# Resident spectra, a third weight buffer and finer pacing in a convolution-plus-MLP kernel

## The chip, the cores and the metric

The kernel runs on one core of a Trainium2 chip. The metric is the device time of one execution in microseconds (us). Before the change the median of three runs is 520.09 us (519.62 to 520.41); the profiled run took 519.61 us, of which 517.8 us lie between the first and the last instruction of the program.

## The reference

The inputs are bfloat16; S = 2048 rows, D = 576 columns, F = 4608. One block of a gated sequence model is computed: an adaptive layer norm, a causal convolution over the whole sequence with a gate, a second adaptive layer norm, and a gated MLP.

```python
def _A_ref(q, k, v, shift_k, ssm_k, ssm_D):
    ...  # k_shift: four shifted copies of k, weighted by shift_k
    kv = k_shift * v
    ...  # y: causal convolution of each column of kv with a filter of 2048 taps (by FFT)
    y = y + kv * ssm_D[None, None, :]
    return q * y

def _B_ref(x, w1, w3, w2):
    gate = jnp.einsum('bsd,df->bsf', x, w1)
    up = jnp.einsum('bsd,df->bsf', x, w3)
    h = _silu(gate) * up
    return jnp.einsum('bsf,fd->bsd', h, w2)

mod = (_silu(c) @ w_mod)            # six rows: sa, ca, ga, sb, cb, gb
h = _layernorm(x) * (1 + ca) + sa
x = x + ga * _A_ref(h, A_k, A_v, A_shift_k, A_ssm_k, A_ssm_D)
h = _layernorm(x) * (1 + cb) + sb
x = x + gb * _B_ref(h, B_w1, B_w3, B_w2)
```

## The kernel before

The 2048 rows are cut into 8 blocks of 256 rows for the convolution and into 4 row blocks r of 512 rows for the MLP. The convolution is done block against block: each block s of kv gets a spectrum X[s], each block of the filter a spectrum V[s] (both 128 x 3456 bfloat16 in SBUF, 864 KB), by matmuls with cosine and sine matrices (`forward2`, lines 304 and 318). The spectrum of output block s is z[s], the sum of X[i]*V[s-i] over i. Each product of that sum is made by `pair` on VectorE: a multiply (L420; L414 for the first) and an add (L422). `real_parts` (L534 to L541) folds z, `inverse` (L554) turns it back by matmuls, `residual` (L568, L569) adds it to x.

The MLP of row block r runs on TensorE: `stream` makes gate and up (L949 over four full chunks of D, L960 over the last 64 rows), ScalarE evicts them (L968, L970), VectorE multiplies (L971), and `down` multiplies by w2 (L1061) in two column halves h, whose results VectorE takes out of PSUM with `og` (L1078). Row block 3 uses `stream_halves` (L1016).

While TensorE works on row block r, the convolution of blocks 2r+2 and 2r+3 is fed in as a generator of small steps, each with a cost in us. After each piece of MLP work `advance` takes as many steps as the budget allows. A negative cost in `mix` is a wait that is filled with steps of another generator.

```python
HEAD = 8
HEAD_PACE = 1.8
CONV_US = (72.0, 97.0, 108.0)
FIRST_DUE = 12.0
# pools: X has 3 buffers, V has 4, wst (w1/w3 chunks) 2 + wst[2], which is also the memory of w2 (w2m)

def x_sums(self, s):
    X = self.X[s]
    self.nc.vector.tensor_add(X[:, 0:6:3, :], X[:, 1:6:3, :], X[:, 2:6:3, :])
    if 3 < s < NBLK - 2:
        self.keep_x(s)                    # X[4], X[5] are written to DRAM
    yield 0.75

def old_x(self, i, s):
    return self.X[i] if s == 2 or s == 4 and i > 0 else self.get("X", i)   # get: 864 KB from DRAM

def old_v(self, i, s):
    return self.V[i] if i >= s - 4 and s < 6 or i >= 4 else self.get("V", i)

def ln_sums(self, src, i, ssum, ssq, col=None):
    col = i if col is None else col
    for func, scale, out in ((ACT.Copy, -1.0 / D, ssum), (ACT.Square, D ** -0.5, ssq)):
        junk = self.lnp.tile([P, D], BF16, name="junk", tag="junk")
        self.nc.scalar.activation(junk[:], src[:, i, :], func, scale=scale, accum_out=out[:, col:col + 1])  # L452

def outcome(self, s, fill, waits, between=None, quick=False):
    def steps():
        yield self.real_parts(s)
        yield -waits[0]
        ...                               # inverse(s, 0), inverse(s, 1) on TensorE, y on ScalarE
        yield -waits[1]
        self.residual(s, y)
        yield 1.5
        if between is not None:
            between()
        ...
            for i in range(2):
                with self.behind(nc.scalar):
                    self.ln_sums(self.xo[s], i, *sums)
                yield 0.0
            yield -waits[2] / 2
            stats = self.ln_var(*sums, "l2")
            yield -waits[2] / 2
            scales = self.ln_shift(*stats)
            yield -3.0
            for cc in range(2):
                self.normed_act(s, cc, *scales)
                yield -1.0
        yield -waits[3]
    yield from self.mix(steps(), fill)

def conv(self, s0):                       # s0 = 2, 4, 6; s1 = s0 + 1
    ...
    def old():
        V, X = self.old_v(s0 - 1, s0), self.old_x(1, s0)
        yield from self.pair(X, V, s0, s0 == 2)
        for j in range(2, s0):
            X = self.old_x(j, s0)
            yield from self.pair(X, V, s1)
            V = self.old_v(s0 - j, s0)
            yield from self.pair(X, V, s0)
        self.V1 = V
        yield from self.gate_stats(s0)
        yield from self.kv_rows(s0)
        ...
    yield from self.mix(filters(), old())
    ...                                   # X0, V0, x_spectrum(s0), X1; pairs with block s0
    def more():
        yield from self.pair(self.X1, self.V[s0], s1, True)
        yield from self.pair(self.X[s0], self.V1, s1)
    def others():
        yield from self.kv_rows(s1)
        self.gate_shift(s1)
        yield from self.mix(self.x_spectrum(s1), more())
        yield from self.x_sums(s1)
    yield from self.outcome(s0, others(), (5.0, 4.5, 6.0, 0.0), lambda: self.gate_rows(s1))
    yield from self.pair(self.X[s1], V0, s1)
    ...
    yield from self.outcome(s1, ahead, (5.0, 4.5, 5.0, 0.0), lambda: self.turn_all(s0))

def advance(self, cost):
    self.due += cost
    while self.due > 0 and self.steps is not None:
        c = next(self.steps, None)
        if c is None:
            self.steps = None
            break
        self.due -= c
        self.spent += c

# down: after chunk 5 of the second half, the rest of the steps, then the transposes of the next rows
                if h == 1 and f0 // W2C == 5 and r + 1 < NRB:
                    self.end()
                    self.turn_all(2 * r + 3)

# row_blocks, r > 0: w1/w3 chunk fc of row block r goes to one of two buffers
                jobs = [(fc, 0, RB, (r + fc) % 2, ...) for fc in range(NF // FC)]
```

Of the kernel before, what the change touches and what calls it, by code (L numbers as in the profile page):

```python
# [34 lines left out]
HEAD = 8  # L35
HEAD_PACE = 1.8
EPS = 1e-5
# [9 lines left out]
class _Kernel:  # L47
    def __init__(self, ctx, tc, q, k, v, shift_k, ssm_k, ssm_D, w1, w3, w2, c, w_mod, out):
# [20 lines left out]
        self.w13, self.kept = {}, {}  # L69
        self.gets = 0  # L70

    def ps(self, shape=(P, 2, 512), dtype=F32):
# [283 lines left out]
    def x_sums(self, s):  # L356
        X = self.X[s]
        self.nc.vector.tensor_add(X[:, 0:6:3, :], X[:, 1:6:3, :], X[:, 2:6:3, :])
        if 3 < s < NBLK - 2:
            self.keep_x(s)  # L360
        yield 0.75
# [71 lines left out]
    def old_x(self, i, s):  # L433

        return self.X[i] if s == 2 or s == 4 and i > 0 else self.get("X", i)

# [11 lines left out]
    def ln_sums(self, src, i, ssum, ssq, col=None):  # L448
        col = i if col is None else col
        for func, scale, out in ((ACT.Copy, -1.0 / D, ssum), (ACT.Square, D ** -0.5, ssq)):  # L450
            junk = self.lnp.tile([P, D], BF16, name="junk", tag="junk")
            self.nc.scalar.activation(junk[:], src[:, i, :], func, scale=scale, accum_out=out[:, col:col + 1])  # L452

# [189 lines left out]
    def first_block(self):  # L643
# [53 lines left out]
        self.mod_piece(2)  # L697
        self.ln_sums(x1, 0, sums[0], sums[1], 0)
        scales = [self.ln_shift(*self.ln_var(*sums, "l1")), (rstd, nmr)]
# [51 lines left out]
    def outcome(self, s, fill, waits, between=None, quick=False):  # L751


        def steps():
# [67 lines left out]
    def conv(self, s0):  # L822
# [13 lines left out]
        def old():  # L836
            V, X = self.old_v(s0 - 1, s0), self.old_x(1, s0)
            yield from self.pair(X, V, s0, s0 == 2)
            for j in range(2, s0):
                X = self.old_x(j, s0)  # L840
                yield from self.pair(X, V, s1)
                V = self.old_v(s0 - j, s0)
                yield from self.pair(X, V, s0)
            self.V1 = V
            yield from self.gate_stats(s0)
# [7 lines left out]
        def beside():  # L853
# [236 lines left out]
    def end(self):  # L1090
        self.advance(1e9)

# [22 lines left out]
    def row_blocks(self, n1):  # L1115
        for r in range(NRB):
# [17 lines left out]
            else:  # L1134
                spills = {1: (self.keep_x, 1), 2: (self.keep_v, 0), 4: (self.keep_v, 1)} if r == 1 else {}
                jobs = [(fc, 0, RB, (r + fc) % 2, (lambda f, i: lambda: f(i))(*spills[fc]) if fc in spills else None)
                        for fc in range(NF // FC)]
# [59 lines left out]
```

## Time and profile before

| view | value |
|---|---|
| median time | 520.09 us |
| span of the profiled run, instructions | 517.8 us, 9255 |
| TensorE (PE) busy | 498.4 us, 96% |
| VectorE (DVE) busy | 345.5 us, 67% |
| ScalarE (ACT) busy | 292.9 us, 57% |
| DMA moved | 107.80 MB, mean 208 GB/s |
| stages, from the lines in the timeline | start 0 to 35 us; row block 0 to 172; row block 1 to 292; row block 2 to 408.6; row block 3 to the end |

A stage is told by where the MLP lines L949 and L1061 begin and end. TensorE runs its instructions in program order, so a matmul of the convolution that waits for VectorE also stops the MLP matmuls behind it. A busy share says how much of a stretch an engine worked; what a change may save on TensorE is first of all its idle time.

### The profile page before, as it was taken

What the parts mean: (1) busy time and instruction counts of PE and PEld (TensorE: products, weight loads), DVE (VectorE), ACT (ScalarE), POOL (GpSimd) and SP (SyncE); (2) the same over time, 40 slices, a digit from 0 to 9 for tenths busy, and PEclk for the clock granted to TensorE, in tenths of its full rate; (3) what the DMA queues carried; (4) which work ended last, traced back from release to release, by engine and by line L of the source; (5) the groups of instructions that cost most, each with busy time, mean ns of one, the idle gap of its engine ahead of it and who ended that gap; (6) DMA issues with size and microseconds to landing.
All of it is one profiled execution on the core that took longest, in us unless ns stands there. A gap on an engine that the chain in (4) does not pass through costs nothing.

```text
span 517.8 us, 9255 instructions
## 1 busy us (share of the span) xinstructions
PE 498.4 (96%) x3650; PEld 294.8 (57%) x3650; DVE 345.5 (67%) x557; ACT 292.9 (57%) x581; POOL 26.1 (5%) x75
## 2 busy tenths in 40 slices
PE   7999989889989999899999999999999999999997
PEld 3667765456868544343677644434587644444775
DVE  8888799999997287989999637998711222221012
ACT  5748689649254488577641467958651355555000
POOL 3100000000000001000001000000100000000000
PEclk9999999989999999999999999999999999999999
DMA  8947959646998696688788549653655535532462
GB/s 262 331 151 210 308 178 289 203 143 221 315 342 270 207 312 230 214 284 289 230 270 280 161 147 361 200 173 91 184 147 151 161 107 176 175 110 77 117 181 69
DMA packets 102207, 107.80 MB, mean 208 GB/s; under 512 B 5075, under 2 KB 94228, under 8 KB 102164
## 3 DMA queue, kind: packets, MB, share of 16 engines
q1 hardware_dynamic: 102142, 107.21, 66.5%
q8 instruction: 28, 0.46, 0.4%
q14 instruction: 15, 0.12, 0.1%
q10 hardware_dynamic: 22, 0.01, 0.0%
HBM read 96.00 MB, written 11.21 MB: 207 GB/s over the span
## 4 chain that ended last, share of the span: by engine, by line
PE 70%; DVE 20%; DMA 4%; ACT 3%; issue 2%; POOL 1%; SPq 0%; DVEq 0%; POOLq 0%; ACTq 0%
PE ps L949 24%; PE ps L1061 22%; PE ps L1016 14%; PE ps L960 4%; DVE p L420 3%; DMA wst<-in_B_w_dram 3%; DVE z L422 3%; DVE h L971 2%; PE ps L318 2%; DVE z L414 1%; DVE kv L342 1%; DVE kvt L341 1%; PE ps L253 1%; DMA knat<-in_A_ssm_k_dram 1%; ACT junk L452 1%
## 5 line engine op out<-in xcount | busy, mean ns | idle before, releaser
L949 PE MATMUL ps<-h2T,wst 128*128 128x512 bf16 (+1 forms) x1056 | 201.1, 341 | 1.9 <-DMA wst<-in_B_w_dram 0.9
L949 PEld LDWEIGHTS <-wst 128*128 128x128 bf16 x1056 | 100.3, 98 | 87.7 <-issue 14.8
L1061 PE MATMUL ps<-wst,h 128*128 128x288 bf16 x1152 | 145.1, 286 | 2.4 <-DVE og L1078 1.4
L1061 PEld LDWEIGHTS <-h 128*128 128x128 bf16 x1152 | 112.3, 98 | 32.0 <-issue 3.1
L968 ACT ACTIVATE h<-ps 128x512 bf16<-128x512 f32 x108 | 65.2, 603 | 64.7 <-PE ps L960 40.8
L1016 PE MATMUL ps<-h2T,wst 64*128 64x512 bf16 x648 | 70.1, 376 | 0.0
L970 ACT CAST u<-ps 128x512 bf16<-128x512 f32 x108 | 63.7, 590 | 0.0
L971 DVE TENSOR_TENSOR h<-h,u 128x512 bf16<-128x512 bf16 x108 | 44.5, 417 | 24.6 <-ACT u L970 24.6
L420 DVE TENSOR_TENSOR p<-X,V 128x3456 bf16<-128x3456 bf16 x28 | 54.6, 1951 | 2.0 <-DMA X<-Xd 1.8
L422 DVE TENSOR_TENSOR z<-z,p 128x3456 bf16<-128x3456 bf16 x28 | 54.6, 1950 | 0.2
L1016 PEld LDWEIGHTS <-wst 64*128 64x128 bf16 x648 | 31.5, 94 | 38.4 <-DMA wst<-in_B_w_dram 0.4
L1031 DVE TENSOR_TENSOR h<-h,u 128x512 bf16<-128x512 bf16 x36 | 15.3, 425 | 54.9 <-ACT u L1030 54.9
L1078 DVE TENSOR_TENSOR og<-ps,gbrow 128x288 bf16<-128x288 f32 x32 | 13.1, 449 | 50.5 <-PE ps L1061 50.5
L1028 ACT ACTIVATE h<-ps 128x512 bf16<-128x512 f32 x36 | 21.5, 598 | 36.2 <-PE ps L1016 36.2
L452 ACT ACTIVATE junk<-x 128x576 bf16<-128x576 bf16 x54 | 37.1, 687 | 0.5
L616 ACT ACTIVATE h2T<-ps,sbcol,cbcol 128x256 bf16<-128x256 bf16 x35 | 16.7, 569 | 34.6 <-PE ps L586 34.6
L960 PE MATMUL ps<-h2T,wst 64*128 64x512 bf16 (+1 forms) x264 | 32.9, 341 | 0.0
L581 ACT ACTIVATE h2row<-x,l2n,l2r 128x576 bf16<-128x576 bf16 (+1 forms) x24 | 14.0, 660 | 13.4 <-DVE l2n L466 13.4
L1030 ACT CAST u<-ps 128x512 bf16<-128x512 f32 x36 | 20.9, 581 | 0.0
L960 PEld LDWEIGHTS <-wst 64*128 64x128 bf16 x264 | 8.5, 94 | 21.0 <-issue 19.9
L341 DVE TENSOR_TENSOR kvt<-kh,shk 128x1152 bf16<-128x1152 bf16 x24 | 18.1, 752 | 0.9 <-DMA kh<-in_A_k_dram 0.6
L342 DVE TENSOR_TENSOR kv<-kv,kvt 128x1152 bf16<-128x1152 bf16 x24 | 18.1, 754 | 0.4
(140 smaller groups left out, 389.5 us busy)
## 6 DMA issues: line engine op xcount, KB each, us to landing
wst<-in_B_w_dram SPq DMA_DIRECT2D x80, 512.0 KB, 4.3
wst<-in_B_w_dram SPq DMA_DIRECT2D x72, 288.0 KB, 3.6
X<-Xd SPq DMA_DIRECT2D x8, 864.0 KB, 7.1
Xd<-X SPq DMA_DIRECT2D x6, 864.0 KB, 5.2
wst<-in_B_w_dram SPq DMA_DIRECT2D x80, 64.0 KB, 3.3
kh<-in_A_k_dram SPq DMA_DIRECT2D x7, 720.0 KB, 6.4
Vd<-V SPq DMA_DIRECT2D x4, 864.0 KB, 8.1
V<-Vd SPq DMA_DIRECT2D x4, 864.0 KB, 6.4
```

Of the source, the lines that this page charges most:

```text
L341: nc.vector.tensor_mul(tmp[:], kh[:, 3 - j:5 - j, :], tap(j))
L342: nc.vector.tensor_add(kv[:], kv[:], tmp[:])
L420: nc.vector.tensor_mul(p[:], X[:], V[:])
L422: nc.vector.tensor_add(z[:], z[:], p[:])
L452: self.nc.scalar.activation(junk[:], src[:, i, :], func, scale=scale, accum_out=out[:, col:col + 1])
L949: nc.tensor.matmul(gus[k][:, i, a * n:(a + 1) * n], w[:, 5 * i + ct, (fi + a) * P:(fi + a + 1) * P], hT[:, ct, t0:t1], start=(first and ct ...
L960: nc.tensor.matmul(gus[k][:, i, a * n:(a + 1) * n], w[rows, 4, (fi + a) * P:(fi + a + 1) * P], hT[rows, 4, t0:t1], start=(first and a == 0 ...
L968: nc.scalar.activation(h3, gus[k][:, 0, :].rearrange("p (a t) -> p a t", a=m), ACT.Silu)
L970: nc.scalar.copy(u[:], gus[k][:, 1, :])
L971: nc.vector.tensor_mul(h3, h3, u[:].rearrange("p (a t) -> p a t", a=m))
L1016: nc.tensor.matmul(gus[f][:, i, :], w[rows, 5 * i + ct if ct < 4 else 4, cols], hT[rows, ct, :], start=swap == 0 and ct == 0, stop=swap == ...
L1061: nc.tensor.matmul(acc[t], self.h3[:, f0 + f, t * P:(t + 1) * P], w[:, f, :], start=(f0 + f == 0), stop=(f0 + f == NF - 1))
```

## The change

The change has several parts. The spectra X[4] and X[5] are no longer written to DRAM and read back: they stay in two of the three X buffers, and for blocks 6 and 7 the products are made with the X index falling and the V index rising, so that X[5] and X[4] are used first and V[4], V[5] last. In row blocks 1 and 2 the memory of w2 serves as a third buffer for w1/w3 chunks until chunk 5. The four statistics passes of each layer norm become steps of their own with a cost, with a pause of the feeding after each second one; `advance` feeds at most 5 us of steps at a time. The first wait of `outcome(2)` grows from 5 to 9, one product is pulled ahead of the spectrum of the odd block, and the pace at the head of row blocks 1 and 2 falls from 1.8 to 1.4. It is meant to cut DMA traffic, to load weights earlier, and to keep bursts of fed work from stopping TensorE.

```diff
-HEAD_PACE = 1.8
+HEAD_PACE = 1.4
...
     def x_sums(self, s):
...
-        if 3 < s < NBLK - 2:
-            self.keep_x(s)
         yield 0.75
...
-        return self.X[i] if s == 2 or s == 4 and i > 0 else self.get("X", i)
+        return self.X[i] if s == 2 or s == 4 and i > 0 or i >= 4 else self.get("X", i)
...                                       (ln_sums)
-            self.nc.scalar.activation(junk[:], src[:, i, :], func, scale=scale, accum_out=out[:, col:col + 1])
+            with self.behind(self.nc.scalar):
+                self.nc.scalar.activation(junk[:], src[:, i, :], func, scale=scale, accum_out=out[:, col:col + 1])
+            self.pause = self.halves or func == ACT.Square      # halves stays False
+            yield 0.4
...                                       (gate_stats)
-            with self.behind(self.nc.scalar):
-                self.ln_sums(self.xo[s], i, ssum, ssq)
-            yield 0.8
+            yield from self.ln_sums(self.xo[s], i, ssum, ssq)
...                                       (outcome)
-                    with self.behind(nc.scalar):
-                        self.ln_sums(self.xo[s], i, *sums)
-                    yield 0.0
+                    yield from self.ln_sums(self.xo[s], i, *sums)
...                                       (conv, old: new branch for s0 = 6)
+            else:
+                V, X = self.old_v(1, s0), self.old_x(s0 - 1, s0)
                 yield from self.pair(X, V, s0)
-            self.V1 = V
+                for j in range(2, s0):
+                    V = self.old_v(j, s0)
+                    yield from self.pair(X, V, s1)
+                    X = self.old_x(s0 - j, s0)
+                    yield from self.pair(X, V, s0)
+                self.X1 = X
...                                       (conv, beside)
-            self.X1 = self.old_x(1, s0)
+            if s0 < NBLK - 2:
+                self.X1 = self.old_x(1, s0)
+            else:
+                self.V1 = self.old_v(1, s0)
...                                       (conv, others)
-            yield from self.mix(self.x_spectrum(s1), more())
+            rest = more()
+            yield next(rest)
+            yield from self.mix(self.x_spectrum(s1), rest)
             yield from self.x_sums(s1)
-        yield from self.outcome(s0, others(), (5.0, 4.5, 6.0, 0.0), lambda: self.gate_rows(s1))
+        yield from self.outcome(s0, others(), (9.0 if s0 == 2 else 5.0, 4.5, 6.0, 0.0), lambda: self.gate_rows(s1))
...                                       (advance)
         self.due += cost
-        while self.due > 0 and self.steps is not None:
+        left = self.due - 5.0
+        while self.due > max(left, 0.0) and self.steps is not None:
...
+            if self.pause:
+                self.pause = False
+                break
...                                       (end)
-        self.advance(1e9)
+        while self.steps is not None:
+            self.advance(1e9)
...                                       (row_blocks, r > 0)
-                jobs = [(fc, 0, RB, (r + fc) % 2, ...
+                bufs = [b if b == 2 else (r + b) % 2 for b in (0, 1, 2, 0, 1, 2, 0, 1, 0)]
+                jobs = [(fc, 0, RB, bufs[fc], ...
```

More of the change, by code (lines that the diff above doesn't have):

```diff
@@ L70, in __init__ @@
         self.gets = 0
+        self.halves = self.pause = False
     def ps(self, shape=(P, 2, 512), dtype=F32):
@@ L697, in first_block @@
         self.mod_piece(2)
-        self.ln_sums(x1, 0, sums[0], sums[1], 0)
+        self.run_all(self.ln_sums(x1, 0, sums[0], sums[1], 0))
         scales = [self.ln_shift(*self.ln_var(*sums, "l1")), (rstd, nmr)]
@@ L836, in old @@
         def old():
[L837 to L842, printed above, removed]
-                yield from self.pair(X, V, s0)
-            self.V1 = V
+            if s0 < NBLK - 2:
+                V, X = self.old_v(s0 - 1, s0), self.old_x(1, s0)
+                yield from self.pair(X, V, s0, s0 == 2)
+                for j in range(2, s0):
+                    X = self.old_x(j, s0)
+                    yield from self.pair(X, V, s1)
+                    V = self.old_v(s0 - j, s0)
+                    yield from self.pair(X, V, s0)
+                self.V1 = V
+            else:
+                V, X = self.old_v(1, s0), self.old_x(s0 - 1, s0)
+                yield from self.pair(X, V, s0)
+                for j in range(2, s0):
+                    V = self.old_v(j, s0)
+                    yield from self.pair(X, V, s1)
+                    X = self.old_x(s0 - j, s0)
+                    yield from self.pair(X, V, s0)
+                self.X1 = X
             yield from self.gate_stats(s0)
@@ L860, in beside @@
                 yield from self.pair(X0, self.V[s0], s0)
-            self.X1 = self.old_x(1, s0)
+            if s0 < NBLK - 2:
+                self.X1 = self.old_x(1, s0)
+            else:
+                self.V1 = self.old_v(1, s0)
             self.gate_rows(s0)
@@ L1135, in row_blocks @@
                 spills = {1: (self.keep_x, 1), 2: (self.keep_v, 0), 4: (self.keep_v, 1)} if r == 1 else {}
-                jobs = [(fc, 0, RB, (r + fc) % 2, (lambda f, i: lambda: f(i))(*spills[fc]) if fc in spills else None)
+                bufs = [b if b == 2 else (r + b) % 2 for b in (0, 1, 2, 0, 1, 2, 0, 1, 0)]
+                jobs = [(fc, 0, RB, bufs[fc], (lambda f, i: lambda: f(i))(*spills[fc]) if fc in spills else None)
                         for fc in range(NF // FC)]
```

## The prediction

> **What bounds the kernel now.** I began with the engine table and the 40 slices of the page, to see which engine is full and whether its clock held.
>
> ```profile
> PE 498.4 (96%) x3650; PEld 294.8 (57%) x3650; DVE 345.5 (67%) x557; ACT 292.9 (57%) x581; POOL 26.1 (5%) x75
> ...
> PE   7999989889989999899999999999999999999997
> ...
> DVE  8888799999997287989999637998711222221012
> ...
> PEclk9999999989999999999999999999999999999999
> ```
>
> TensorE (PE) is full; it idles for 517.8 - 498.4 = 19.4 us in all. That is nearly the whole room for a change that takes no matmul away, as this one. One slice (the ninth, 103.6 to 116.5 us) shows a lower clock. VectorE (DVE) is full in the first third only. Next I asked for busy time by stage, to place the 19.4 us.
>
> ```profile
> 0.00:35.00 35.00, 30.61 (x218) 18.54 (x218) 29.67 (x68) 21.71 (x43) 8.08 (x24) 1.00 0.88 275
> 35.00:172.00 137.00, 128.90 (x1047) 91.02 (x1046) 124.39 (x183) 87.87 (x175) 5.23 (x7) 0.99 0.76 239
> 172.00:292.00 120.00, 117.35 (x735) 63.34 (x733) 102.67 (x138) 73.91 (x148) 4.39 (x4) 1.00 0.79 253
> 292.00:408.60 116.60, 116.09 (x722) 62.39 (x722) 66.94 (x114) 70.84 (x143) 5.27 (x4) 1.00 0.59 180
> 408.60:517.80 109.20, 105.49 (x937) 59.52 (x936) 21.84 (x58) 38.54 (x72) 3.17 (x36) 1.00 0.44 130
> ```
>
> The columns are length, then busy us of PE, weight loads, DVE, ACT, POOL, then clock, DMA share and GB/s. PE idles 4.4 us at the start and 3.7 at the end (the last rows' way out; both untouched), 8.1 in row block 0, 2.65 in row block 1, 0.5 in row block 2. So at most 8.1 + 2.65 + 0.5 = 11.3 us can be had, and row block 2, where the resident spectra act, has nothing to give. What ended the idle times is in the waits of PE:
>
> ```profile
> PE ps L554 <- DVE z L540: 3.7, 1, 3.7
> ...
> PE ps L1061 <- DVE og L1078: 1.4, 1, 1.4
> PE ps L318 <- DVE kv L344: 1.3, 1, 1.3
> PE ps L1061 <- DMA wst<-in_B_w_dram: 0.9, 3, 0.4
> PE ps L949 <- DMA wst<-in_B_w_dram: 0.9, 1, 0.9
> ```
>
> The largest is one wait: the inverse of block 2 comes up in PE's program before VectorE has folded z. The timeline places it at 101.8 us, and the windows around it show a second loss:
>
> ```profile
> 105.56 1.12 PE L554 MATMUL ps<-z,Fb 128*128 128x288 bf16 x4 [3.72 <-DVE z L540]
> ```
> ```profile
> 81.22:105.19 23.97, 20.61 (x123) 9.73 (x120) 22.92 (x39) 16.68 (x34) 1.51 (x2) 1.00 0.80 238
> 105.19:108.61 3.42, 2.83 (x12) 1.62 (x13) 3.42 (x6) 1.20 (x2) 0.00 (x0) 0.50 0.29 99
> ```
>
> After the wait the clock stands at 0.50 for 3.42 us; PE is busy for 2.83 us of them with work that takes half of that at full clock, so 1.4 us more are lost. Together with a 0.22 us wait for L541: 3.7 + 0.2 + 1.4 = 5.3 us for one early matmul.
>
> **What the Trainium skill says.** "TensorE: Matmul & The Clock Gate", section "What's actually happening", says that the array falls to half rate after about one idle window of 3.4 us and needs a busy one to return. This trace agrees: 3.72 us of waiting, then 3.42 us at 0.50. So a wait cut below that length should lose its clock penalty too. "Perfetto Trace Analysis", section "Identifying the Most-Contended Engine", warns that PE's busy share is no measure of its distance from the peak. I tested that here: eight L949 matmuls take 1.73 us in the chain, 216 ns each, in the stretches without waits, so nothing large hides inside "busy". "DMA: Bandwidth & Descriptors", section "Issuing engines are not separate DMA queues", says that all transfers share the same 16 engines; so a spill taken away may speed up weights, if the share was high then. In row block 2 the share was 0.59: there it was not.
>
> **The change part by part.**
>
> *The first wait of outcome(2), 5 to 9.* It feeds 4 us more of other steps between the fold and the inverse. At row block 0's rate (72 / (93.5 - 24.7) = 1.05 us of steps per us of MLP) PE gets about 3.8 us more MLP work before the inverse, so it arrives at 101.8 + 3.8 = 105.6; z's L540 ends at 105.4. The wait of 3.7 us and the half-clock stretch should go: up to -5.3 us. But PE then reaches the next meeting earlier: L318 of block 3 starts at 110.68, and kv of block 3 (L344) ends at 110.6. VectorE is busy for 31.05 of the 32 us from 90 to 122 and gets no faster. One VectorE product (1.95 us, L420) that stands before L344 could move behind it, so kv is ready at about 108.7 at the earliest; the product pulled ahead of the spectrum moves L318 back by its cost of 2 us. I expect a wait of 1 to 2 us there, too short for the clock. Kept: about 3.5 us.
>
> *The end of row block 0.* VectorE has work ahead until 161.6 (l2n); ScalarE writes h2row from 161.79 to 164.1, and PE transposes it at 165.01. That is 0.9 us of slack. All that PE gains earlier is given back here unless this chain moves too. It holds slack of its own: z of block 3 is done at 137.6 while its inverse starts at 142.46 (4.9 us), and about 8 us of products and kv rows for the next row block stand in VectorE's queue between y (144.3) and L568 (147.45). Against this, the statistics now cost 1.6 us of budget per outcome (3.2) and the longer wait 4: by the code the steps of this stage come to about 87 us before and 94 after, against a budget of 12 + 24 x 2.15 + 14 x 2.11 = 93 until the rest is forced. So the last steps come in a rush. I let this take 1.5 us of the 3.5. The wait of L1061 for og (1.4, behind a product of the next row block) moves with the queue; I add half of it to the sum below. Row block 0 without it: about -2.
>
> *Third w1/w3 buffer (row blocks 1 and 2).* It covers waits of L949 for weights: 0.9 us, once. The w2 loads then start three chunks before the end (3 x 8.2 us), ample for four buffers. About -0.8, and -0.2 of the 0.4 that L1061 waits at 271.3 as the queue is freer.
>
> *Resident X[4], X[5].* Removes two writes and, by the code, changes 8 X reads and 4 V reads into 5 and 5: four transfers of 864 KB out of 107.8 MB, 3.3%. VectorE waits for X reads 1.8 us in all, off PE's path. With V[4], V[5] held to the end, only one V buffer rotates once V[6] exists, so V[3] cannot be fetched before the product with V[2] has run: some 6 to 8 us of landing may show on VectorE, two or three times. VectorE idles from 293.7 to 303.4 and from 305 to 314 there, so this hides, with a small risk at 346 (inverse of block 6, z done at 343.9). Effect: -0.2 at row block 1's tail, +0.3 risk in row block 2, sum 0.
>
> *Pacing (pause, 5 us cap, HEAD_PACE 1.4, statistics as steps).* No instruction is added. Row block 1's wait of L318 for kv (1.35 us) is where a burst of products stands before L344; thinner feeding may halve it: -0.7. Row block 1 costs 120.0 us against 116.6 for row block 2, which lacks one filter spectrum (about 1.5 us of matmuls), so 1.9 us is all there is. Ten or so small waits elsewhere may shift either way: -0.5 to +1.
>
> Sum: -2 (row block 0) - 1.0 (weights) - 0.7 (kv) + 0 = -3.7; with half of the og wait (-0.9 of 1.8 in all, 152 to 155 us), -4.6. 520.1 - 4.6 = **515.5 us**.
>
> **Rivals.** (1) *VectorE and the h2row chain bound row block 0.* Then the inverse's wait goes and returns at L318, at og or at the transposes; row block 0 stays 137 us. For: 124.4 of 137 us busy, 0.9 us slack at 165. Against: VectorE did work of the next row block in this stage (the first product of block 4 at 119.16). Time: 518 to 519. (2) *Everything moves together*: the whole 5.3 goes, the 1.8 at 152 to 155 us, and the 2.65 of row block 1: 520.1 - 5.3 - 1.8 - 2.65 = 510.3. (3) *DMA bounds the first down half*: the share is 1.02 from 122 to 155 us and L1061 already waited twice for w2; a PE that comes 5 us earlier waits longer for w2. Time: 517. (4) *A new long wait*, on a late V read or on rushed steps, with a clock drop: +3.5 + 1.4, so 521 to 525.
>
> **Range and chances.** The middle of rivals 1 and 2 is my number. The range of 8 in 10 runs from rival 2 to rival 1 with a little of rival 4: 510.3 to 520.3. Faster by over 2% needs under 509.7, more than nearly all of the 11.3 us: 0.06. Slower by over 2% needs two or three new waits of the longest kind: 0.03. Within 2%: 0.91.
>
> **What would show it.** Right: no wait of L554 over 1 us near 105, no clock digit under 9 after the start; row block 0 at 134 to 135.5 us; L949 waits for no DMA; Xd down to 4 writes and 5 reads, Vd up to 5 reads; row block 2 still 116 to 117. Wrong: row block 0 unchanged with waits at L318, og or L586 (rival 1); under 132 us (rival 2); L1061 waiting for w2 over 2 us (rival 3); a second clock dip (rival 4).

## The result and the profile after

The changed kernel takes 523.43 us (median of 4 runs, 522.53 to 524.00) against 519.86 us before: a ratio of 1.0066 with a 95% interval of 1.0046 to 1.0086. It is slower by 3.6 us in the medians, where 515.5 was predicted. The same lines of the page as were shown of before (busy time, then slices for TensorE, VectorE and the clock):

```profile
PE 499.5 (96%) x3630; PEld 296.0 (57%) x3650; DVE 345.4 (66%) x557; ACT 294.3 (56%) x581; POOL 26.1 (5%) x75
...
PE   7999998969997999999999999999899999999996
...
DVE  8887799989988364996989949499732222221011
...
PEclk9999999979999999999999999999999999999999
```

Busy times are within 1.5 us of before, and the clock still dips in the ninth slice. So the loss lies in waits and in the clock. The stages must be cut where they end in each kernel. A part "gate and up" begins with the first L949 matmul of a row block (L966 in the changed file) and a part "down" with its first L1061 (L1078). The windows of before, then of after; the columns are those of the windows shown in the prediction:

```profile
34.28:129.89 95.61, 89.38 (x713) 59.53 (x712) 88.79 (x136) 72.48 (x146) 4.10 (x6) 0.98 0.68 213
129.89:171.44 41.55, 39.60 (x336) 31.39 (x334) 35.76 (x47) 16.04 (x32) 1.13 (x1) 1.00 0.92 294
171.44:254.38 82.94, 80.70 (x426) 34.03 (x424) 67.62 (x103) 60.99 (x122) 2.07 (x3) 1.00 0.79 255
254.38:292.06 37.68, 37.27 (x313) 29.65 (x312) 35.67 (x40) 12.91 (x27) 2.33 (x1) 1.00 0.81 249
292.06:371.09 79.03, 78.52 (x404) 32.33 (x402) 60.95 (x97) 58.55 (x117) 4.58 (x3) 1.00 0.59 189
```
```profile
33.69:131.19 97.50, 90.04 (x711) 60.09 (x713) 88.49 (x134) 70.81 (x142) 4.42 (x5) 0.96 0.66 206
131.19:175.63 44.44, 41.27 (x337) 32.16 (x335) 36.90 (x50) 18.16 (x36) 2.16 (x2) 0.96 0.94 301
175.63:254.98 79.35, 78.18 (x397) 32.41 (x403) 57.87 (x95) 58.56 (x117) 2.45 (x3) 1.00 0.66 208
254.98:294.10 39.12, 39.12 (x336) 31.40 (x335) 36.77 (x41) 15.84 (x31) 2.33 (x1) 1.00 0.73 219
294.10:375.12 81.02, 78.24 (x397) 32.49 (x403) 62.89 (x97) 56.79 (x113) 2.45 (x3) 1.00 0.61 197
```

Row block 0 became 1.9 + 2.9 = 4.8 us longer, the gate and up of row block 1 3.6 us shorter (its down part 1.4 longer, 39.12 against 37.68, since convolution matmuls moved into it, 336 matmuls against 313), and the gate and up of row block 2 2.0 us longer. That is +4.6 in these three row blocks; the start is 0.6 shorter and the rest 0.4 longer, +4.4 in the span. What TensorE waited for in the changed kernel:

```profile
PE ps L319 <- DVE kv L345: 4.0, 1, 4.0
PE ps L966 <- DMA wst<-in_B_w_dram: 2.6, 2, 1.5
PE ps L586 <- ACT h2row L581: 2.4, 1, 2.4
```

The wait of L554 for z is gone, as meant. In its place stands a wait of 4.0 us of the odd block's spectrum (L319) for its kv, and a second new one of the transposes (L586) for the normed rows. Also new are two waits of gate and up (L966) for weights in row block 0, at 44.6 and 81.2 us, 2.6 us together; the kernel before has none there. The timeline and two pairs of windows show where they fall and what the clock did after them:

```profile
109.47 0.64 PE L319 MATMUL ps<-kv,Fb 128*128 128x288 bf16 x2 [4.00 <-DVE kv L345]
...
111.82 2.13 PE L554 MATMUL ps<-z,Fb 128*128 128x288 bf16 x8
...
168.57 0.62 PE L586 MATMUL ps<-ident,h2row 128*128 128x128 bf16 x5 [2.37 <-ACT h2row L581]
```
```profile
107.10:113.95 6.85, 4.48 (x20) 3.02 (x21) 6.82 (x9) 2.26 (x4) 0.00 (x0) 0.52 0.23 62
...
165.00:168.50 3.50, 1.20 (x10) 0.72 (x8) 1.71 (x3) 0.85 (x2) 0.69 (x1) 1.00 1.00 333
168.50:172.00 3.50, 3.43 (x21) 2.39 (x22) 2.94 (x2) 2.24 (x6) 0.00 (x0) 0.54 0.63 225
```

L319 now comes *before* the inverse L554, and needs a later product of VectorE than the inverse does. VectorE finishes the fold of z (L541) and then kv (L345):

```profile
106.91 0.75 DVE L541 TENSOR_TENSOR z<-z 128x1152 bf16<-128x1152 bf16 x1
...
108.58 0.75 DVE L345 TENSOR_TENSOR kv<-kv,vt 128x1152 bf16<-128x1152 bf16 x1
```

**The order of TensorE's program.** The wait lengths follow from where each convolution matmul stands among the MLP matmuls. That can be counted from the program: MLP work that precedes it, at 213 ns per 512 columns (1% under the 216 ns of the chain). In us of MLP work from the start of row block 0:

| kernel | first L318/L319 of block 3 | inverse of block 2 | inverse of block 3 | transposes of block 3 |
|---|---|---|---|---|
| before | 58.3 | 55.7 | 88.6 | 105.7 |
| after | 59.0 | 60.0 | 94.3 | 106.8, 107.5 |

With a wait of 5 the inverse is issued in the middle of the kv steps (0.75 + 3 x 1.5 = 5.25), so in front of the spectrum. With 9 the kv steps (6) and the pulled product (2) do not fill it, so the first matmul of the spectrum is taken as filler and gets in front of the inverse. The inverse of block 2 then stands 4.3 us later and that of block 3 5.7; the transposes of block 3, which are forced out at chunk 5, stand only 1.1 to 1.8 us later, so they come closer behind the work that they need.

### The profile page after: what moved, and what is told of

Its sections match the earlier page's. It is cut to its first block, busy times and chain, and to the rows that moved or that the text cites. A ratio compares the mean times of both kernels' runs of the same rounds, so it can differ in the third digit from the quotient of the medians.

```text
span 522.2 us, 9225 instructions
## 1 busy us (share of the span) xinstructions
PE 499.5 (96%) x3630; PEld 296.0 (57%) x3650; DVE 345.4 (66%) x557; ACT 294.3 (56%) x581; POOL 26.1 (5%) x75
## 2 busy tenths in 40 slices
DMA packets 101631, 104.27 MB, mean 200 GB/s; under 512 B 5011, under 2 KB 94164, under 8 KB 101588
## 4 chain that ended last, share of the span: by engine, by line
PE 70%; DVE 18%; ACT 4%; DMA 4%; issue 2%; POOL 1%; SPq 0%; DVEq 0%; ACTq 0%; POOLq 0%
PE ps L966 25%; PE ps L1078 21%; PE ps L1033 13%; PE ps L977 4%; DVE p L419 3%; DVE z L421 3%; DMA wst<-in_B_w_dram 2%; PE ps L319 2%; DMA kh<-in_A_k_dram 1%; DVE h L988 1%; PE ps L554 1%; DVE kvt L342 1%; ACT junk L452 1%; DVE kv L343 1%; PE ps L254 1%
## 5 line engine op out<-in xcount | busy, mean ns | idle before, releaser
L966 PE MATMUL ps<-h2T,wst 128*128 128x512 bf16 (+1 forms) x1037 | 200.0, 341 | 4.5 <-DMA wst<-in_B_w_dram 2.6
L966 PEld LDWEIGHTS <-wst 128*128 128x128 bf16 x1056 | 100.6, 98 | 89.7 <-issue 14.3
L1078 PE MATMUL ps<-wst,h 128*128 128x288 bf16 x1152 | 146.4, 288 | 0.8 <-DMA wst<-in_B_w_dram 0.8
L1078 PEld LDWEIGHTS <-h 128*128 128x128 bf16 x1152 | 112.8, 98 | 30.6 <-issue 1.8
L452 ACT ACTIVATE junk<-x 128x576 bf16<-128x576 bf16 x54 | 37.2, 690 | 0.6
```

What stands on the lines that cost most here:

```text
L966: nc.tensor.matmul(gus[k][:, i, a * n:(a + 1) * n], w[:, 5 * i + ct, (fi + a) * P:(fi + a + 1) * P], hT[:, ct, t0:t1], start=(first and ct ...
L1078: nc.tensor.matmul(acc[t], self.h3[:, f0 + f, t * P:(t + 1) * P], w[:, f, :], start=(f0 + f == 0), stop=(f0 + f == NF - 1))
```

## The experiments

Two theories at the start. **A:** the longer first wait is the cause: it turns the order round and feeds the end of the stage late. **B:** the pacing (costed statistics steps, pause, cap) is the cause. The lengths of the stages in the profiled run of each kernel, in us, with the ratio to before (95% interval) over all its timed runs; gu is gate and up, dn is down. In row block 2 the down part is 37.47 us in all but the last.

| run | gu0 | dn0 | gu1 | dn1 | gu2 | ratio |
|---|---|---|---|---|---|---|
| before | 95.61 | 41.55 | 82.94 | 37.68 | 79.03 | 1 |
| after | 97.50 | 44.44 | 79.35 | 39.12 | 81.02 | 1.0066 (1.0046 to 1.0086) |
| e1 after, wait 5 | 98.77 | 41.07 | 79.34 | 39.29 | 80.99 | 1.0018 (1.0000 to 1.0035) |
| e2 before, wait 9 | 97.94 | 41.78 | 83.04 | 37.29 | 79.08 | 1.0024 (1.0010 to 1.0038) |
| e3 after, no pacing | 97.46 | 42.32 | 79.04 | 39.07 | 83.67 | 1.0061 (1.0040 to 1.0082) |
| e4 before, resident + third buffer | 96.72 | 41.28 | 81.87 | 38.29 | 80.38 | 1.0002 (0.9984 to 1.0020) |
| e5 before, head 1.4 + third buffer | 95.65 | 41.55 | 78.46 | 39.12 | 79.08 | 0.9952 (0.9931 to 0.9974) |
| e6 before, pull | 97.66 | 40.86 | 82.25 | 37.87 | 80.39 | 1.0015 (1.0001 to 1.0029) |
| e7 before, filler | 95.64 | 41.50 | 82.05 | 37.21 | 80.60 | 1.0000 (0.9979 to 1.0022) |
| e8 after, feed 80 | 100.42 | 40.59 | 79.34 | 39.12 | 80.99 | 1.0044 (1.0025 to 1.0063) |
| e9 after, wait 5, no pull | 98.96 | 40.18 | 79.15 | 39.07 | 80.59 | 0.9997 (0.9980 to 1.0014) |
| e10 before, reordered | 94.47 | 44.38 | 78.62 | 39.12 | 79.07 | 0.9968 (0.9955 to 0.9980) |
| e11 before, pacing | 98.61 | 40.18 | 79.89 | 38.47 | 80.41 | 1.0012 (0.9995 to 1.0030) |
| e12 before, head 1.4 | 96.99 | 42.94 | 78.46 | 39.76 | 79.08 | 0.9942 (0.9926 to 0.9959) |
| e13 e10 + hold | 94.28 | 39.96 | 78.46 | 39.12 | 79.08 | 0.9882 (0.9864 to 0.9901) |
| e14 e12 + hold | 95.63 | 39.60 | 78.46 | 39.12 | 79.07 | 0.9921 (0.9897 to 0.9945) |
| e15 before, head 1.0 | 96.79 | 41.27 | 78.23 | 40.79 | 80.13 | 1.0019 (1.0007 to 1.0031) |

A profiled run is one execution: whether a wait near 104 us is followed by 3.41 or 6.83 us at half clock differs between kernels with the same wait, so a difference of about 1 us in gu0 alone carries no verdict. The same holds for gu2: e7 changes nothing in row block 2 and has the same order of matmuls there, and its gu2 is 80.60 against 79.03 (see e7). So 1.6 us of gu2 without a wait that names its cause carries no verdict either.

### e1: the first wait back at 5

```diff
-        yield from self.outcome(s0, others(), (9.0 if s0 == 2 else 5.0, 4.5, 6.0, 0.0), ...
+        yield from self.outcome(s0, others(), (5.0, 4.5, 6.0, 0.0), ...
```

> The changed kernel with the first wait of outcome(2) put back from 9 to 5, all else as changed. Theory A (the longer wait is the cause: it puts a spectrum matmul of block 3, which needs kv, in front of the inverse of block 2, and it feeds block 3's inverse and layer norm about 7 us later, so that the transposes at the end of row block 0 wait): the 4.0 us wait of L319 for kv and the 2.4 us wait of L586 go, a wait of L554 for z of about 3.7 us returns; row block 0 ends at 171 to 172.5 us instead of 175.6; time 519 to 521. Theory B (the pacing, that is the costed statistics steps, the pause and the 5 us cap, is the cause): the wait of L586 stays and the time stays at 522 to 524.

521.6 us, ratio 1.0018: nearly three quarters of the loss is gone; the wait of L586 for the normed rows of block 3 is gone, and dn0 is 3.4 us shorter. The wait of L554 is back, and longer than before the change (4.9 us, line below), so gu0 grew by 1.3: within the changed kernel, gate and up is no shorter with the old order. Theory A holds for the end of row block 0; but the time is 0.6 us above the range that A gave, and row block 0 ends at 173.2 us and not by 172.5, so something else costs time too.

```profile
PE ps L554 <- DVE z L540: 4.9, 1, 4.9
```

### e2: the longer wait alone

```diff
-        yield from self.outcome(s0, others(), (5.0, 4.5, 6.0, 0.0), ...
+        yield from self.outcome(s0, others(), (9.0 if s0 == 2 else 5.0, 4.5, 6.0, 0.0), ...
```

> The kernel before with only the first wait of outcome(2) raised from 5 to 9. Theory A: L319 for block 3 stands before the inverse of block 2 and waits some 4 us for kv, and the transposes at the end of row block 0 wait 1 to 3 us; time 521.5 to 524. Theory B: no wait at the transposes, the wait of L554 is gone; time 515 to 519.

522.08 us, ratio 1.0024. The longer wait alone makes the kernel slower: L318 stands before the inverse and waits 6.0 us for kv. The end of the stage suffers less than the 1 to 3 us expected (0.8 us at L586, dn0 +0.2). The statistics steps, which put 3.2 us more cost into the budget, are missing here; e3, which lacks them too, also has 0.8 us at L586.

```profile
PE ps L318 <- DVE kv L344: 7.9, 3, 6.0
```

### e3: the pacing undone in the changed kernel

```diff
-            with self.behind(self.nc.scalar):
-                self.nc.scalar.activation(junk[:], ...)
-            self.pause = self.halves or func == ACT.Square
-            yield 0.4
+            self.nc.scalar.activation(junk[:], ...)
...                                    # callers, advance and end() as in the kernel before
```

> The changed kernel with the statistics steps, the pause and the 5 us cap put back as before (waits of 9, HEAD_PACE 1.4, resident spectra and third buffer kept). Theory A: the wait at L319 stays, the one at L586 gets smaller by some 1 to 2 us as 3.2 us of budget per stage are free again; time 521 to 523.5. Theory B: row block 0 ends at 171 us or earlier; time 516 to 520.

524.15 us, ratio 1.0061, the same as the changed kernel within the intervals; 0.65 us above the range that theory A gave. Theory B falls as the cause of the whole loss: without the pacing the loss stays. dn0 is 2.1 us shorter, as A expected, but row block 2 is longer (83.67): L963 there waits 2.5 us for ScalarE, with a half-clock stretch at 365 us.

### e4: resident spectra and third buffer alone

```diff
-        if 3 < s < NBLK - 2:
-            self.keep_x(s)
...                                    # old_x, old() and beside() as in the change
-                jobs = [(fc, 0, RB, (r + fc) % 2, ...
+                bufs = [b if b == 2 else (r + b) % 2 for b in (0, 1, 2, 0, 1, 2, 0, 1, 0)]
+                jobs = [(fc, 0, RB, bufs[fc], ...
```

> The kernel before with only the resident X[4], X[5] (falling order) and the third w1/w3 buffer. Both theories: row block 0 as before, L949 no longer waits 0.9 us for weights in row block 1, row block 2 within 0.5 us of before; time 518 to 520.3. If late reads of V stop VectorE so long that TensorE waits (rival), 521 or more.

520.1 us, ratio 1.0002. The two parts that gave the change its name are worth nothing that these runs resolve. The wait of L949 for weights in row block 1 is gone and gu1 is 1.1 us shorter, but dn1 is 0.6 and gu2 1.35 longer: in its place L369, the first convolution matmul of row block 2, waits 1.3 us for VectorE's og. That row block 2 would stay within 0.5 us was a miss.

### e5: head pace 1.4 and third buffer

```diff
-HEAD_PACE = 1.8
+HEAD_PACE = 1.4
...                                    # bufs as in e4
```

> The kernel before with only the third w1/w3 buffer and HEAD_PACE 1.4 (no resident spectra, no pacing, waits of 5). Theory: row block 0 as before; in row block 1 the gate-and-up part falls from 82.9 to 79.3 us, as in the changed kernel (79.35), because the spectra of block 4 come 7 us of MLP work later and TensorE meets VectorE less; row block 2 keeps its 79.0 or loses up to 0.5. Time 517 to 518.5. Rival (the gain of row block 1 comes from the resident spectra or the statistics steps): gate-and-up of row block 1 stays over 81.5, time 519 to 520.5.

517.1 us, ratio 0.9952. gu1 falls to 78.46, all of the gain that row block 1 shows in the changed kernel. The gain is had without resident spectra and without the statistics steps.

### e6: the pull alone

```diff
-            yield from self.mix(self.x_spectrum(s1), more())
+            rest = more()
+            yield next(rest)
+            yield from self.mix(self.x_spectrum(s1), rest)
```

> The kernel before with only the one product pulled ahead of the odd block's spectrum. If the pull is what makes L319 wait at 366 us in the changed kernel (1.7 us, row block 2 2.0 us longer): gate-and-up of row block 2 rises from 79.0 to 80.5 or more. If not: all stages within 0.5 us of before, time 519.3 to 520.5.

521.15 us, ratio 1.0015: a small loss that the interval just clears, and above the 520.5 of the "if not". gu2 is 80.39, just short of the 80.5 expected if the pull is at fault; the lengthening alone is no more than e7 shows without a pull, so the verdict rests on the wait. gu0 is 2.0 us longer, with 6.83 us at half clock where the kernel before has 3.41; how much of that is the pull stays open. The timeline of ScalarE shows it: the spectrum of block 7 now comes while the statistics passes (L452, 0.86 us each with their read-out) run between the evictions, and TensorE waits 1.73 us for ScalarE to evict a spectrum:

```profile
358.38 0.67 ACT L452 ACTIVATE junk<-x 128x576 bf16<-128x576 bf16 x1
...
359.04 0.61 ACT L320 CAST X<-ps 128x576 bf16<-128x576 f32 x1
```
```profile
359.70 0.40 PE L318 MATMUL ps<-kv,Fb 128*128 128x288 bf16 x2 [1.73 <-ACT X L320]
```

### e7: filler matmuls before the inverse

```diff
+            if s == 2:
+                self.warm(12, self.h2T[0][:, 0, :])      # 12 matmuls of 512 columns, result unused
             for cc in range(2):
                 nc.scalar.copy(y[:, cc, :]..., self.inverse(s, cc)[:, :, 0:H])
```

> The kernel before with twelve matmuls of 512 columns that compute nothing needed, placed right before the inverse of block 2, so that TensorE is busy for about 2.6 us of the 3.7 us it waits for z. They tell the clock's share from the wait's: if the half-clock stretch costs time of its own, it goes, and the kernel gets 1.2 to 2.5 us faster with the work unchanged (517.5 to 518.8). If the half clock costs nothing beside the wait, or the filler is itself in the way, 519.5 to 520.5.

519.96 us, ratio 1.0000. The half-clock stretch is gone and TensorE's recorded waiting there shrinks to 1.27 us. The stage is as long as before: gu0 95.64 against 95.61.

```profile
101.01 2.75 PE L641 MATMUL ps<-h2T,ident 128*128 128x512 bf16 x12
105.04 0.65 PE L554 MATMUL ps<-z,Fb 128*128 128x288 bf16 x4 [1.27 <-DVE z L540]
...
110.17 0.66 PE L318 MATMUL ps<-kv,Fb 128*128 128x288 bf16 x4 [0.85 <-DVE kv L344]
```

The time saved by the full clock is waited for at the next meeting, L318 for kv, at 110.17; before, the same matmul started at 110.68 without a recorded wait. Row block 0 began 0.53 us earlier here (33.75 against 34.28), so counted from its start both stand at 76.4 us. The half clock cost nothing at this point, and nothing at the end of the stage. In this stretch VectorE sets the time. The executions of this kernel with no more half clock than the profiled one (mean clock 0.999 or 1.000, 8 of 14) have a median of 519.2 us, those of the kernel before with one such stretch (0.997, 18 of 49) 519.4.

In row block 2, which is the same in both, TensorE came 1.9 us earlier here (290.14 against 292.07), but a spectrum X read from DRAM landed only 0.3 us earlier: VectorE waited for it until 313.96 (before, 0.47 us until 314.28), worked on from there almost without a break, and TensorE lost 2.07 us at kv, where it had lost 0.51.

```profile
313.96 1.96 DVE L420 TENSOR_TENSOR p<-X,V 128x3456 bf16<-128x3456 bf16 x1 [2.08 <-DMA X<-Xd]
```
```profile
347.54 0.41 PE L318 MATMUL ps<-kv,Fb 128*128 128x288 bf16 x2 [2.07 <-DVE kv L344]
```

### e8: faster feeding in the changed kernel

```diff
-CONV_US = (72.0, 97.0, 108.0)
+CONV_US = (80.0, 97.0, 108.0)
```

> The changed kernel with CONV_US[0] raised from 72 to 80, so the steps of row block 0 are fed 11% faster; waits and pacing as changed. In TensorE's program the inverse of block 3 then stands 7.7 us of MLP work earlier (86.6 instead of 94.3). Theory (late feeding makes the end of row block 0 wait): the down part of row block 0 falls from 44.4 to 41.0 to 41.8 us and the wait at L586 goes. In the same program L319 for kv of block 3 stands 3.3 us earlier, in front of the inverse, so its wait grows to about 6 to 8 us and gate-and-up rises to 98.5 to 100.5. Time 522 to 524. If the down part stays over 43, the late feeding is not the cause.

522.84 us, ratio 1.0044. Both halves came, dn0 even below its range: dn0 40.59 with no wait at L586, and 8.0 us of waiting of L319 for kv, gu0 100.42. A rival for dn0 is that TensorE only came later, after the longer wait. Counted from the start of row block 0, ScalarE has the normed rows of block 3 ready at 131.2 us against 136.3 in the changed kernel, and TensorE comes to their transposes at 133.5 against 132.5. So the rows, 5.1 us earlier, decide, and not TensorE's 1.0 us: the late feeding is shown to be what stops the end of the stage. That L319 in front of L554 makes the wait for kv is shown too, here and in e2.

```profile
PE ps L319 <- DVE kv L345: 8.0, 1, 8.0
```

### e9: wait back at 5 and no pull

```diff
-        ... (9.0 if s0 == 2 else 5.0, 4.5, 6.0, 0.0) ...
+        ... (5.0, 4.5, 6.0, 0.0) ...
-            rest = more()
-            yield next(rest)
-            yield from self.mix(self.x_spectrum(s1), rest)
+            yield from self.mix(self.x_spectrum(s1), more())
```

> The changed kernel with the first wait of outcome(2) back at 5 and without the product pulled ahead (pacing, HEAD_PACE 1.4, resident spectra, third buffer kept). If the longer wait and the pull are the two culprits: down of row block 0 at 41.0 to 41.6 us, gate-and-up of row block 2 at 79.0 to 79.8 without the 1.7 us wait of L319, row block 1 still about 118.5; time 517 to 519. If a third part costs time (the pacing in row block 0, where the run with the wait at 5 had 98.8 us of gate-and-up): row block 0's gate-and-up stays at 97 or more and the time is 519 to 521.

520.35 us, ratio 0.9997. The loss is gone with these two, but the gain of row block 1 does not show in the total, because a third part costs: gu0 is 98.96 (1.7 us of waits for weights, 5.0 us for z), and gu2 80.59, where L319 still waits 1.4 us for ScalarE.

### e10: a better order for the inverse and the spectrum

```diff
-HEAD_PACE = 1.8
+HEAD_PACE = 1.4
-CONV_US = (72.0, 97.0, 108.0)
+CONV_US = (76.0, 97.0, 108.0)
...                                    # bufs as in e4
-            yield from self.mix(self.x_spectrum(s1), more())
+            rest = more()
+            if s0 == 2:
+                yield next(rest)
+                yield next(rest)
+            yield from self.mix(self.x_spectrum(s1), rest)
-        ... (5.0, 4.5, 6.0, 0.0) ...
+        ... (8.0 if s0 == 2 else 5.0, 4.5, 6.0, 0.0) ...
```

> A version meant to be better than both: the kernel before with HEAD_PACE 1.4, third buffer, and in row block 0 alone both steps of the first product pulled ahead, a first wait of 8 and CONV_US[0] 76. In TensorE's program the inverse of block 2 stands 2.5 us of MLP work later than before, kv of block 3 comes after it by another 1.7 us, and the inverse of block 3 and the transposes stay where they were. Theory (order, not only delay, decides): waits of 1 to 2.5 us at L554 and at L318, none long enough for the half clock; gate-and-up of row block 0 at 93.5 to 95 us, down at 41 to 42; time 514.5 to 516.5. Rival (VectorE bounds row block 0 whatever TensorE's order): the stage as long as before, 137 us, time 516.5 to 518.

518.5 us, ratio 0.9968: slower than e5 in its median, and above both expected ranges (514.5 to 516.5, and 516.5 to 518 for the rival). gu0 is 94.47 as expected, with no wait of L554 and 2.2 us of L318. But dn0 is 44.38: the og wait grew to 3.3 us.

```profile
PE ps L1065 <- DVE og L1082: 3.3, 1, 3.3
```

og begins at 153.59 us here, at 153.86 in the kernel before. TensorE came earlier and waited at the same place. What stands ahead of og in VectorE's queue in this run are products of block 4, for the next row block:

```profile
147.84 1.95 DVE L422 TENSOR_TENSOR z<-z,p 128x3456 bf16<-128x3456 bf16 x1
...
151.05 1.95 DVE L420 TENSOR_TENSOR p<-X,V 128x3456 bf16<-128x3456 bf16 x1
152.92 0.75 DVE L323 TENSOR_TENSOR W<-W,Wo 128x1152 bf16<-128x1152 bf16 x1
153.59 0.82 DVE L1082 TENSOR_TENSOR og<-ps,gbrow 128x288 bf16<-128x288 f32 x2
```

### e11: the pacing alone

```diff
...                                    # ln_sums, gate_stats, outcome, advance and end as in the change; all else as before
```

> The kernel before with only the pacing: statistics passes as costed steps, the pause after each second, the 5 us cap. If the pacing is a cost of its own in row block 0: gate-and-up of row block 0 rises from 95.6 to 97 to 99 us with a longer wait of L554 for z, time 521 to 523. If it is neutral without the longer wait: within 0.5 us stage by stage, 519.3 to 520.7. If it helps as meant (fewer bursts before TensorE): 517 to 519.

520.7 us, ratio 1.0012 with 1 inside the interval: no clear effect, just at the edge of "neutral". By stages it is not neutral: gu0 +3.0 and gu2 +1.4 against dn0 -1.4 and gu1 -3.0. In row block 0, L953 (gate and up) waits 1.9 us for weights, two waits that the kernel before does not have, and L556 (the inverse) 4.8 us for z, 1.1 us more than before: together the 3.0 us of gu0. Why these waits come is open.

```profile
PE ps L953 <- DMA wst<-in_B_w_dram: 1.9, 2, 1.0
```

The 3.0 us of gu1 are had at the old head pace, with the pacing alone.

### e12: head pace alone

```diff
-HEAD_PACE = 1.8
+HEAD_PACE = 1.4
```

> The kernel before with only HEAD_PACE 1.4. It splits the gain of the run that had this and the third buffer: if the head pace carries it, gate-and-up of row block 1 is 79 to 80 us and the time 517 to 518.3; if the third buffer carries it, 82 or more and 519.3 to 520.5.

516.93 us, ratio 0.9942, gu1 78.46 as with the third buffer. One constant is enough for the gain. In TensorE's program, counted as above from the start of row block 0, it moves the spectrum of block 4 from 128.5 to 135.4 and the inverse of block 4 from 156.7 to 162.7 us; the 1.35 us wait for kv is gone, and with it the wait for weights, also without a third buffer.

### e13 and e14: next row block's products held behind og

To e10 (e13) and to e12 (e14):

```diff
+    def held(self, s, last):
+        if s in (4, 5) and not last:
+            return self.tc.issue_after(self.mark)
+        return self.placed(last)
...                                    # pair(): both multiplies use held(s, last)
...                                    # down(), after the four og of the first half of row block 0:
+                if r == 0 and h == 0 and t == 3:
+                    self.mark = [i for i in nc.cur_bb.bb.instructions if i.engine == nc.vector.engine][-1]
```

> The version of e10 with the products of blocks 4 and 5 held back on VectorE until og of the first half of row block 0 has been issued. If og's place in the queue is what stops TensorE: the 3.3 us wait of L1065-like matmuls for og falls under 0.5 us, down of row block 0 falls from 44.4 to 41 to 42 us, time 515 to 516.8. If VectorE's total work is the bound: the wait comes back at the transposes of block 3 or in row block 1 (gate-and-up over 80), time 517.5 to 519.

> The kernel before with HEAD_PACE 1.4 and the same hold. Place in the queue: the 1.8 us wait for og goes, down of row block 0 at 41 or less, time 515 to 516.3 (1 to 2 us under e12). Total work: no faster than e12 (516.9), with new waits in row block 1.

e13: 514.03 us, ratio 0.9882. e14: 515.42 us, ratio 0.9921. The wait for og is gone in both; dn0 falls by 4.4 and 3.3 us to 39.96 and 39.60, in e13 more than expected, and e13 is a microsecond under its range. The work that VectorE owes to this stage is not its bound; the order is. In e13 VectorE is even idle 0.58 us before og, which starts at 147.36, 6.2 us earlier than in e10:

```profile
147.36 0.82 DVE L1088 TENSOR_TENSOR og<-ps,gbrow 128x288 bf16<-128x288 f32 x2 [0.58 <-PE ps L1071]
```

Its row block 0 is one stretch at full clock:

```profile
33.39:127.67 94.28, 88.45 (x710) 59.04 (x712) 85.36 (x134) 71.61 (x145) 4.55 (x6) 1.00 0.72 221
127.67:167.63 39.96, 39.53 (x336) 31.39 (x334) 34.24 (x44) 16.74 (x33) 1.07 (x1) 1.00 0.96 311
```

This version beats the kernel before by 1.2% and the changed one by 1.8% (514.03 against 523.43 us).

### e15: a still lower head pace

```diff
-HEAD_PACE = 1.8
+HEAD_PACE = 1.0
```

> The kernel before with HEAD_PACE 1.0. If TensorE gains by meeting VectorE later: gate-and-up of row block 1 at 78 to 79, as with 1.4 or 0.3 less, since no wait over 0.5 us is left there to remove; time 516 to 517.5. If later meetings crowd the end of the stage: a wait at the transposes of block 5 or 7 shows and the time is 518 or more.

520.91 us, ratio 1.0019. gu1 gains another 0.2 us and the rest loses: dn1 40.79, gu2 80.13, dn2 39.30. The convolution is pushed into the down part, where new waits of 0.5 to 1.3 us appear. Of the three values tried, 1.4 is the best.

## Why the prediction was wrong, point by point

*The bound and the room.* Right: TensorE is full, row block 2 had nothing to give, and the whole room in waits was 11.3 us. e13 took 5.9 us without removing a matmul. "The middle of rivals 1 and 2 is my number" is a slip: the middle of 518.5 and 510.3 is 514.4, not 515.5.

*The first wait of outcome(2).* This is the step that failed: "I expect a wait of 1 to 2 us there, too short for the clock. Kept: about 3.5 us." The time of arrival was as said (101.8 + 3.8 = 105.6; measured 105.47), but by luck, for it holds 2.6 us of waits for weights that I had not foreseen. I placed L318 2 us later than before, behind the inverse, and it came first. kv was ready at 109.3 instead of 108.7. The wait was 4.0 us, and 6.85 us at 0.52 of the clock followed. In place of 3.5 us kept, gu0 lost 1.9. e2 shows it without the rest (6.0 us for kv, gu0 +2.3); e8, which moves L319 further forward, makes it 8.0. The code had it: a fill of 9 cannot be met by 6 + 2, so a spectrum matmul is taken as filler. Still, the order is not all of gu0: the pacing alone lengthens it by 3.0 (e11), and with both it is 1.9 and not the sum. Time that TensorE has already lost to weights it does not wait for again at kv, 2.6 + 4.0 us in the changed kernel against 6.0 in e3, which has the longer wait without the pacing. Rival 4, "*A new long wait*" with a clock drop, at 521 to 525, is what came: the one at L586 "on rushed steps" as it said, the larger one at L319 from the order, which it did not name.

*The price of the clock.* "3.7 + 0.2 + 1.4 = 5.3 us for one early matmul" was wrong as a gain: e7 removed the half-clock stretch and moved nothing, and in e13, where the wait of L554 and the half clock are both gone, gu0 is only 1.3 us shorter. Where VectorE sets the time of the next meeting, a faster TensorE gains nothing. Rival 1 said so; it was right in that, and wrong in its reason: in e13 and e14 row block 0 takes 134.2 and 135.2 us in place of 137.2 once og no longer stands behind the next row block's products; that place in the queue held the stage. I had seen those products, but misplaced them: "about 8 us" stand ahead of L568 from 139.48 on, and only 3.1 us of them behind y (144.3).

*The end of row block 0.* The mechanism was right (94 us of steps against a budget of 93, 0.9 us of slack at the transposes) and the size was off: "I let this take 1.5 us". Measured: 2.37 us at L586, then a half-clock window in which TensorE was busy 3.43 us, so 1.7 us more, 4.1 in all, less 1.4 of og wait that went. dn0 +2.9. e1, e2, e3 and e8 order it: the inverse of block 3 at 94.3 us of MLP work gives dn0 44.4, at 92.4 (e3, e2) 42.3 and 41.8, at 88.5 (e1) 41.1, at 86.6 (e8) 40.6. It is not the only thing that sets dn0: in e10 it stands at about 88 and dn0 is 44.4, from og.

*Third buffer and resident spectra.* Bytes were right: 107.80 to 104.27 MB, 4 writes, 5 and 5 reads. "About -0.8 and -0.2" was wrong: e4 is level with before, and e5 is no better than e12. The wait of L949 for weights was there, but another wait took its place. And X reads are not always "off PE's path": in e7 TensorE's 2.07 us at kv in row block 2 go back to one.

*Pacing.* "-0.7" for row block 1 was too small: the head pace alone gives 4.5 us of gu1, 2.4 net of the longer dn1 (e12), and the pause, the cap and the costed statistics alone give 3.0, 2.3 net (e11). Either is enough, and the changed kernel, with both, has 2.15 net. So "1.9 us is all there is" was too low as well. In row block 0 I had given the pacing no cost; there it has 1.6 us (e11: gu0 +3.0, dn0 -1.4), and over the whole kernel no clear effect. I missed row block 2: +2.0 us there, where I had "sum 0". TensorE waits 1.7 us there for ScalarE, where statistics passes and the spectrum of block 7 meet; e6 shows that wait with the pull alone, and e9, without the pull, still 1.4.

*What the sum would be.* Taken out of the changed kernel, the longer wait carries about 0.48 of the 0.66% (e1, 1.0018) and the pull about 0.21 more (e9, 0.9997). Put alone into the kernel before, they cost 0.24 (e2) and 0.15 (e6). Each of these figures has about 0.2 either way, and the two ways of counting do not agree in the wait: its loss is larger beside the pacing, with which the end of row block 0 gives way too (dn0 +2.9 against +0.2 in e2). What is left open: why the pacing lengthens the wait for z from 3.7 to 4.8 us and brings weight waits in row block 0; only that it does is shown (e11).

## What to carry to other kernels

Before moving a matmul of a side task in TensorE's program, list the order of all its meetings with the engine that feeds it; a delay that lets the next meeting slip in front trades one wait for a longer one. A wait removed is a gain only if the engine waited for is not the one that sets the next meeting too: look at what stands ahead of that next product in its queue (e7, e10). Work that a scheduler draws forward into an idle engine is free only behind the instructions that the full engine needs next (e13, e14). To say what a part of a change is worth, take it out of the new kernel and also put it alone into the old one; here the longer wait had 0.48% by the first and 0.24% by the second.

## What the hardware showed that was not expected

"TensorE: Matmul & The Clock Gate", section "What's actually happening", speaks of an idle window of about 3.4 us. Here half-clock stretches came in whole windows, of 3.41 (before), 6.83 (after, at 107.4 us) or 10.24 us (e8, at 103.5 us), and after shorter waits than that: after 2.37 us (the changed kernel, 168.8 us), and in e12 after 1.81 us, shown below, with TensorE busy for 1.57 us in the 3.4 us ahead. The same wait, 2.22 us of the spectrum for kv, was followed by 3.41 us at 0.50 in e10 and by none in e13, with TensorE busy for 1.18 us of 3.4 us ahead in both (shown second). So "a wait cut below that length should lose its clock penalty" was too safe; by these runs a wait of 1.8 to 2.4 us may or may not have one.

```profile
152.30:155.70 3.40, 1.57 (x12) 0.99 (x11) 3.40 (x6) 3.37 (x8) 0.00 (x0) 1.00 0.89 314
155.70:159.10 3.40, 3.40 (x17) 2.14 (x16) 3.40 (x8) 1.79 (x6) 0.00 (x0) 0.51 0.19 59
```
```profile
105.90:109.30 3.40, 1.18 (x11) 0.82 (x10) 3.40 (x6) 1.07 (x2) 0.00 (x0) 1.00 0.57 170
109.37:112.78 3.41, 3.19 (x9) 1.13 (x8) 3.41 (x3) 1.18 (x2) 0.00 (x0) 0.50 0.42 144
...
105.50:108.90 3.40, 1.18 (x12) 0.84 (x10) 3.40 (x6) 1.07 (x2) 0.00 (x0) 1.00 0.52 150
108.90:112.30 3.40, 3.35 (x19) 1.41 (x19) 3.40 (x3) 1.99 (x4) 0.00 (x0) 1.00 0.55 189
```
